# Position bias read bank by bank in the first block of a chunk, and two weight conversions one step sooner

## The chip, the cores and the metric

The program runs on one core of one Trainium2 chip. The metric is the device time of one execution in microseconds (us); the figure given is the median of several executions.

## The reference

Attention with a learned position bias, followed by a gated feed-forward layer (called MoE in the code, though there is one expert). Sizes: 4 batches, 8 heads, 576 positions, head width 64, 32 hidden units in the bias network, 2304 tokens, model width 512, inner width 1536. All inputs and outputs are float32.

```python
scores = q @ k.T / sqrt(64)
x = log1p(|i - j|) / log1p(max(i, 1))          # 576 x 576
bias = relu(x[..., None] @ w1 + b1) @ w2       # 576 x 576 x 8 heads
attn = softmax(scores + bias) @ v
x = attn, heads side by side                   # 2304 x 512
out = (sigmoid(x @ w_gate) * (x @ w_val)) @ w_out
```

## The kernel before

Three stages follow each other on the core: the position bias (up to about 115 us), attention (to about 348 us) and the MoE stage (to the end). Each engine works its instructions off in the order in which the program lists them; in all three stages this order is written out by hand (`tc.manual_schedule()`), and the tile framework adds a semaphore wait wherever an instruction uses a tile that another engine has written or read.

**The bias stage** (`bias`). Each hidden unit of the bias network is on or off at a position pair, so the bias is x times one sum over units plus another sum. The key positions are cut into 9 chunks of 64 (`NCH`; numbered 0 to 8 here), the query positions into 5 blocks of 128, taken in the order 0, 1, 4, 2, 3 (`BORD`). For each chunk and block TensorE sums the 0/1 tiles `ind` and `far` with the coefficients `cfs` into the PSUM tile `bps` (`sums`, L455). `bps` has two banks; bank a holds one half of the chunk's columns, and in each bank the first 256 values per partition are the sum that is multiplied by x, the other 256 the sum that is added. Two such tiles exist, so block 4, the third of a chunk, can start only when block 0 of that chunk has been read. `leave` (L457) empties a block. VectorE multiplies the first sums by x into `btmp` (L463). Then there are two ways for the second sums:

- blocks 1, 2 and 3: VectorE reads them and writes the bias itself (L474);
- block 0 of chunks 0 to 7 (`BPOOL`) and block 4: ScalarE copies them, scaled, to `brest` (L466), and GpSimd adds `brest` and `btmp` (L469). For block 4 the program lists ScalarE's read first and VectorE's read (L480) second.

Between these, ScalarE makes the `ind` tiles of the next chunk (L436, from the PSUM tile `y` that TensorE writes at L431), VectorE makes the `far` tiles (L449), a conversion of MoE weights runs on both (`cvm`; L229 on ScalarE, L232 to L241 on VectorE), and in chunks 3 to 6 TensorE adds 20 matmuls on the values of one batch to block 4 (`gram`, L379), which are loaded by DMA through GpSimd's queue.

**The MoE stage** (`Moe.run`). 24 steps, written in the string `ORDER`: A0 A1 B0 A2 B1 A3 ... (numbered 0 to 23). A step computes gate and value sums of one slice f of the inner width for one part of 384 tokens (TensorE L1024 into `pg` and `pu`); ScalarE takes the sigmoid (L1033), VectorE multiplies (L1034), ScalarE rounds the product to `gh` (L1035), VectorE subtracts for the rest `gl` (L1036). One step later TensorE multiplies `gh` and `gl` with the output weights (L1048, into `po`). `pg` and `pu` have one buffer each.

Weights are split in two parts before use, in tiles of 128x512: tile 3f+z is gate (z=0), value (z=1) or output weights (z=2) of slice f. ScalarE writes the upper part (L978) and, for a scale needed later, the sum of its squares (L997); VectorE writes the lower part (L987). Tiles 0 to 8 were converted in the bias stage, so for them this is all; tiles from 9 on first go through L229 (ScalarE), L232, L235, L238 and L241 (VectorE). Tile n is begun when its turn comes (`begin`): every step calls `convert`, which begins the next raw tile, moves the tiles already begun by one stage, and issues the load of another raw tile (`stage`, L955 or L958). Steps 2, 3, 4 and 9 call it once more (`EXTRA`). Ahead of that, the three strings of `START` say by hand what is done before step 0 and in steps 0 and 1: `s` issues one load from ScalarE's queue, `w5` does the next action of tile 5 (the sixth tile): first the upper part, then the lower part.

Of the kernel before, what the change touches and what calls it, by code (L numbers as in the profile page):

```python
# [15 lines left out]
AF = mybir.ActivationFunctionType  # L16
ALU = mybir.AluOpType

B, H, S, D = 4, 8, 576, 64
# [5 lines left out]
NCH = S // 64  # L25
# [11 lines left out]
BPOOL = (0,)  # L37
# [8 lines left out]
PRE = lambda f, z: f < 3  # L46
ORDER = "A0 A1 B0 A2 B1 A3 B2 A4 B3 A5 B4 A6 B5 A7 B6 A8 B7 A9 B8 A10 A11 B9 B10 B11"
CONV = (2, 1)
START = 'w2 w3 w3 w2 w4 s w4 s', 's s s s', 'w5 w5'
PLAN = {  # L50
# [195 lines left out]
def bias(tc, v, small, steps, lpos, xtab, lx, biases, biasL, ident, level, sizes, moe, begun):  # L246
# [4 lines left out]
    nc = tc.nc  # L251
    PSUM = bass.MemoryType.PSUM
    with ExitStack() as ph:
# [36 lines left out]
        ps = pp.tile([128, 2, 2, H, 32], F32, name="bps").rearrange("p a b h j -> p a (b h j)")  # L290
# [22 lines left out]
        for z, (o, col) in enumerate(((wl, 3), (wt, 7))):  # L313
            nc.vector.tensor_tensor(
                out=o, in0=wr[:, z].rearrange("p (o m) -> p o m", o=1).to_broadcast([128, 4, HID]),
                in1=pk[:, col:col + 4].rearrange("p (g o) -> p g o", o=1).to_broadcast([128, 4, HID]), op=ALU.mult)
        nc.vector.tensor_tensor(out=wl, in0=wl, in1=wt, op=ALU.add)
        for part in range(3):
# [9 lines left out]
            out=wy, in0=wt.rearrange("p (o g) m -> p o (g m)", o=1).to_broadcast([128, 4, 128]),  # L328
            in1=group.rearrange("p (r o) -> p r o", o=1).to_broadcast([128, 4, 128]), op=ALU.mult)
# [5 lines left out]
        for ab in range(2):  # L335
            nc.gpsimd.tensor_tensor(
                out=cf[:, ab], in0=w2r.rearrange("p (h o) -> p h o", o=1).to_broadcast([128, H, 4]),
                in1=group.rearrange("p (o g) -> p o g", o=1).to_broadcast([128, H, 4]), op=ALU.mult)
# [3 lines left out]
        total, cup, cun = (cp.tile([128, 1], F32, name=n) for n in ("ctotal", "cup", "cun"))  # L342
# [112 lines left out]
                nc.tensor.matmul(out=o, lhsT=st, rhs=cfs[:, part], start=(part == 0), stop=(part == 1))  # L455

        def leave(ps, c, blk):  # L457
            n = 2 if blk < 4 else 1
            tmp = tp.tile([128, 2, H, 32], F32, name="btmp")[:, 0:n]
            js = slice(64 * c, 64 * c + 64)  # L460
            if blk < 4:
                x = xt[:, blk, js].rearrange("p (s o j) -> p s o j", s=2, o=1)
                nc.vector.tensor_tensor(out=tmp, in0=ps[:, :, 0], in1=x.to_broadcast([128, 2, H, 32]), op=ALU.mult)  # L463
            if blk in BPOOL and c < NCH - 1 or blk == 4:
                rest = tp.tile([128, 2, H, 32], F32, name="brest")[:, 0:n]
                nc.scalar.activation(out=rest, in_=ps[:, 0:n, 1], func=AF.Copy, scale=cun)  # L466

                def put(out, in0, in1):
                    nc.gpsimd.tensor_tensor(out=out, in0=in0, in1=in1, op=ALU.add)  # L469
            else:  # L470
                rest = ps[:, 0:n, 1]

                def put(out, in0, in1):
                    nc.vector.scalar_tensor_tensor(out=out, in0=in0, scalar=cun, in1=in1, op0=ALU.mult, op1=ALU.add)  # L474
            if blk < 4:
                for t, h0, h1 in ((biases[0], 0, 6), (biases[1], 6, 8)):
                    put(t[:, :, blk::4, 32 * c:32 * c + 32], rest[:, :, h0:h1], tmp[:, :, h0:h1])
                return
            x = xt[:, 4, 64 * c:64 * c + 32].rearrange("p (o j) -> p o j", o=1)
            nc.vector.tensor_tensor(out=tmp[:, 0], in0=ps[:, 0, 0], in1=x.to_broadcast([128, H, 32]), op=ALU.mult)  # L480
            for s_ in range(2):
                r = slice(64 * s_, 64 * s_ + 64)
                for e in range(2):
                    put(biasL[64 * e:64 * e + 64, :, s_, 32 * c:32 * c + 32], rest[r, 0, e::2], tmp[r, 0, e::2])
# [16 lines left out]
        for c in range(NCH):  # L501
# [11 lines left out]
            for n, blk in enumerate(BORD):  # L513
                ps = pp.tile([128, 2, 2, H, 32], F32, name="bps")
# [322 lines left out]
class Moe:  # L837
# [442 lines left out]
    def run(self):  # L1280
# [4 lines left out]
        with ExitStack() as ph, tc.manual_schedule():  # L1285
# [14 lines left out]
            self.un, self.fits = {}, []  # L1300
            self.do(START[0], nc.scalar)
            before, opened = [], False
            for i, (c, f) in enumerate(order):
# [19 lines left out]
                if i < 2:  # L1323
                    self.do(START[1 + i], nc.scalar)
                for s in stored:
# [69 lines left out]
```

## Time and profile before

| | |
|---|---|
| median of 3 runs | 773.50 us (773.39 to 773.68) |
| the profiled execution, its own time | 772.53 us |
| its span, from first to last instruction | 770.7 us |
| TensorE busy | 716.0 us, 93% |
| VectorE busy | 630.3 us, 82% |
| ScalarE busy | 547.2 us, 71% |
| GpSimd busy | 343.2 us, 45% |
| mean granted TensorE clock over the span | 0.987 of full speed |

The profile is of one execution. A busy share is an average over three stages with different limits, so it says little of an edit in one stage; for that the timelines and the waits of the stretch in question are read. The bias stage lies at 12 to 115 us, the first steps of the MoE stage at 348 to 390 us. In a timeline a row gives the start, the duration, the engine, the line and the tiles (out<-in); in square brackets stands how long the engine had been idle and what it waited for.

### The profile page before, as it was taken

Reading aid. Unit: us, or ns where it says so; the run is one execution under the profiler, and the core shown is the slowest. Engines: PE = TensorE matmul, PEld = TensorE weight load, DVE = VectorE, ACT = ScalarE, POOL = GpSimd, SP = SyncE. Lnnn points to the kernel's source line nnn. Section 1 sums busy time; section 2 is a strip of 40 time slices with the busy share of each in tenths; the row PEclk is TensorE's granted clock in tenths of the full one; section 3 lists DMA queues with packets and bytes.
Section 4 is the critical chain, followed back from the end, with each engine's and each line's share of the span. In section 5 each row is a group of like instructions: output and inputs, shape, how many; then the busy total and the mean of one; then the engine's idle time right before and its main releaser. Section 6 shows DMA issues by size and latency. Waiting matters only on the chain.

```text
span 770.7 us, 16565 instructions
## 1 busy us (share of the span) xinstructions
PE 716.0 (93%) x6058; PEld 519.8 (67%) x6058; DVE 630.3 (82%) x1336; ACT 547.2 (71%) x1189; POOL 343.2 (45%) x436
## 2 busy tenths in 40 slices
PE   6877858999999998989999999999999999999997
PEld 3766746777777776769898999955555555555553
DVE  6788887999999999973789898879888886777662
ACT  5987737989889898875667565777766667566653
POOL 4343456998989999891000000125423340534200
PEclk9999987999999999999999999999999999999999
DMA  6387424878899789888687523345222213412102
GB/s 197 134 187 201 128 82 94 170 167 191 176 168 195 158 202 221 201 198 282 210 278 232 175 98 109 128 158 181 82 83 72 66 55 114 151 47 73 56 1 82
DMA packets 128593, 111.77 MB, mean 145 GB/s; under 512 B 78848, under 2 KB 99456, under 8 KB 128512
## 3 DMA queue, kind: packets, MB, share of 16 engines
q1 hardware_dynamic: 124480, 105.15, 50.0%
q0 software_dynamic: 2112, 2.62, 2.3%
q10 hardware_dynamic: 1920, 2.95, 1.1%
q8 instruction: 47, 0.77, 0.4%
q14 instruction: 34, 0.28, 0.1%
HBM read 76.08 MB, written 18.95 MB: 123 GB/s over the span
## 4 chain that ended last, share of the span: by engine, by line
PE 60%; DVE 9%; ACT 8%; DMA 3%; issue 3%; POOL 1%; SPq 0%; ACTq 0%; DVEq 0%; POOLq 0%
PE po L1048 16%; PE pg L1196 10%; PE pu L1196 7%; PE pg L1024 6%; PE pu L1024 6%; PE acc L768 5%; PE sc L660 4%; PE pt L705 3%; DVE en L676 3%; ACT at L590 3%; ACT en L681 2%; DVE at L591 2%; PE sc L649 1%; DMA vr<-in_v_dram 1%; DMA wo<-scratch 1%
## 5 line engine op out<-in xcount | busy, mean ns | idle before, releaser
L1154 POOL TENSOR_TENSOR ws<-wm 128x256 f32<-128x256 f32 x44 | 43.1, 979 | 283.6 <-DMA xt<-xs 145.1
L1196 PEld LDWEIGHTS <-wv 128*128 128x128 f16 x1008 | 98.0, 98 | 83.1 <-issue 8.2
L681 ACT ACTIVATE en<-en,mn 128x576 f32<-128x576 f32 x144 | 110.7, 774 | 17.0 <-DVE mn L676 16.6
L1196 PE MATMUL pg<-xq,wv 128*128 128x384 f16 x576 | 109.3, 326 | 2.5 <-ACT c L1222 2.1
L676 DVE CUSTOM_DVE_ANT_1 en<-sc,bias 128x576 f32<-128x576 f32 x128 | 91.7, 754 | 10.7 <-PE sc L660 10.2
L699 POOL TENSOR_TENSOR cr<-en,cr 128x512 f16<-128x512 f32 x124 | 90.0, 748 | 5.2
L1048 PE MATMUL po<-wo,gh 128*128 128x512 f16 x288 | 85.6, 379 | 0.0
L1196 PE MATMUL pu<-xq,wv 128*128 128x384 f16 x432 | 82.0, 326 | 1.1 <-DVE c L1202 0.9
L660 PE MATMUL sc<-k,part 64*128 64x288 f32 x768 | 77.3, 319 | 2.8 <-DVE bias L474 1.4
L591 DVE SCALAR_TENSOR_TENSOR at<-pt,at 128x512 f16<-128x512 f32 (+3 forms) x132 | 72.0, 565 | 7.9 <-ACT at L590 6.3
L1202 DVE TENSOR_TENSOR c<-pu,c 128x384 f32<-128x384 f32 x72 | 39.9, 554 | 42.7 <-PE pu L1196 28.0
L660 PEld LDWEIGHTS sc<-k,part 64*128 64x128 f32 x768 | 60.5, 191 | 19.0 <-issue 13.1
L590 ACT ACTIVATE at<-pt 128x512 f16<-128x512 f32 (+3 forms) x132 | 61.6, 493 | 9.5 <-PE pt L705 8.2
L768 PE MATMUL acc<-at,vv 128*64 128x288 f16 x868 | 65.8, 289 | 2.7 <-ACT xe L772 1.1
L455 PE MATMUL bps<-cfs,ind 128*128 128x64 f16 x972 | 52.6, 194 | 14.1 <-DVE bias L474 7.8
L436 ACT ACTIVATE ind<-y 128x576 bf16<-128x576 f32 x100 | 60.5, 650 | 6.4 <-PE y L431 5.8
L1214 ACT ACTIVATE gh<-c 128x384 f16<-128x384 f32 x48 | 25.1, 522 | 54.0 <-DVE c L1212 52.5
L455 PEld LDWEIGHTS <-ind 128*128 128x128 bf16 x972 | 45.4, 99 | 23.1 <-issue 10.8
L705 PE MATMUL pt<-ident,en 128*128 128x128 f32 x328 | 53.4, 286 | 7.8 <-ACT en L681 5.0
L768 PEld LDWEIGHTS <-vv 128*64 128x64 f16 x896 | 48.1, 109 | 17.2 <-issue 14.5
L1024 PE MATMUL pg<-xhi,w 128*128 128x384 f32 x192 | 53.9, 339 | 1.2 <-DVE w L987 1.0
L1048 PE MATMUL po<-wo,gl 128*128 128x512 f16 x144 | 54.6, 379 | 0.0
(194 smaller groups left out, 1678.3 us busy)
## 6 DMA issues: line engine op xcount, KB each, us to landing
wm<-scratch SPq DMA_DIRECT2D x48, 256.0 KB
scratch<-wm SPq DMA_DIRECT2D x27, 256.0 KB
wo<-scratch SPq DMA_DIRECT2D x24, 256.0 KB
qr<-in_q_dram SPq DMA_DIRECT2D x16, 320.0 KB
vr<-in_v_dram SPq DMA_DIRECT2D x16, 320.0 KB
kr<-in_k_dram SPq DMA_DIRECT2D x16, 288.0 KB
xs<-xe SPq DMA_DIRECT2D x16, 288.0 KB
xrec<-rs SPq DMA_DIRECT2D x48, 96.0 KB
```

The costliest lines, as they stand in the source:

```text
L455: nc.tensor.matmul(out=o, lhsT=st, rhs=cfs[:, part], start=(part == 0), stop=(part == 1))
L590: nc.scalar.activation(out=hi, in_=ps, func=AF.Copy, scale=float(2.0 ** up))
L591: return lambda: nc.vector.scalar_tensor_tensor(out=lo, in0=ps, scalar=float(2.0 ** up), in1=hi, op0=ALU.mult, op1=ALU.subtract)
L660: nc.tensor.matmul(out=pair[h][:, e, 0:HF], lhsT=qs[rows, l, 128 * it:128 * it + 128], rhs=ks[rows, r, HF * e:HF * e + HF], start=(i == 0) ...
L676: nc.vector.tensor_tensor_reduce(out=half(en), in0=ps[:, :, 0:HF], in1=nbias, scale=-0.125, scalar=3.0e38, op0=ALU.add, op1=ALU.min, accum ...
L681: nc.scalar.activation(out=en, in_=en, func=AF.Exp, bias=mn, scale=-1.0, accum_out=sm)
L699: nc.gpsimd.tensor_tensor(out=t[:, a:a + z.stop - z.start], in0=en[:, z], in1=t[:, z], op=ALU.subtract)
L705: nc.tensor.transpose(pt[:, J], en[:, 128 * J:128 * J + 128], ident)
L768: nc.tensor.matmul(out=acc[D * h:D * h + D, 0:HF], lhsT=vv[:, h, J, z], rhs=at[:, h, y, cs], start=(i == 0), stop=(i == len(mms) - 1))
L1024: self.nc.tensor.matmul(out=(pg, pu)[z], lhsT=l, rhs=r, start=(kc == 0 and i == 0), stop=(kc == 3 and i == 2))
L1048: self.nc.tensor.matmul(out=po, lhsT=l[:, tt], rhs=r, start=(first and i == 0), stop=(last and i == 2))
L1196: nc.tensor.matmul(out=p, lhsT=W[i][:, l, at + kc], rhs=V[b][:, r, kc], start=(new and n == 0), stop=(n == 5), skip_group_check=not new)
```

## The change

It has two parts.

1. In `leave`, for block 0 of chunks 0 to 7 (`apart`), VectorE's one read of 512 values (L463) becomes two of 256, one for each bank, and ScalarE's one copy of 512 values (L466) becomes two of 256. They are listed in turn: VectorE bank 0, ScalarE bank 0, VectorE bank 1, ScalarE bank 1. In the changed kernel these are L469 and L470. Block 4 runs through the same loop with one round, as before.
2. In `START`, `w5 w5` moves from step 1 to step 0 of the MoE stage, behind the four loads that ScalarE's queue issues there.

```diff
-START = 'w2 w3 w3 w2 w4 s w4 s', 's s s s', 'w5 w5'
+START = 'w2 w3 w3 w2 w4 s w4 s', 's s s s w5 w5', ''
...
         def leave(ps, c, blk):
-            n = 2 if blk < 4 else 1
+            n, apart = 2 if blk < 4 else 1, blk in BPOOL and c < NCH - 1
             tmp = tp.tile([128, 2, H, 32], F32, name="btmp")[:, 0:n]
             js = slice(64 * c, 64 * c + 64)
             if blk < 4:
                 x = xt[:, blk, js].rearrange("p (s o j) -> p s o j", s=2, o=1)
-                nc.vector.tensor_tensor(out=tmp, in0=ps[:, :, 0], in1=x.to_broadcast([128, 2, H, 32]), op=ALU.mult)
-            if blk in BPOOL and c < NCH - 1 or blk == 4:
+                if not apart:
+                    nc.vector.tensor_tensor(out=tmp, in0=ps[:, :, 0], in1=x.to_broadcast([128, 2, H, 32]), op=ALU.mult)
+            if blk == 4 or apart:
                 rest = tp.tile([128, 2, H, 32], F32, name="brest")[:, 0:n]
-                nc.scalar.activation(out=rest, in_=ps[:, 0:n, 1], func=AF.Copy, scale=cun)
+                for a in range(n):
+                    if apart:
+                        nc.vector.tensor_tensor(out=tmp[:, a], in0=ps[:, a, 0], in1=x[:, a].to_broadcast([128, H, 32]), op=ALU.mult)
+                    nc.scalar.activation(out=rest[:, a], in_=ps[:, a, 1], func=AF.Copy, scale=cun)
```

The change moves instructions at two places, shown as the built programs list them. Line numbers behind L457 are larger by 4 in the changed kernel.

The first place is block 0 of chunk 1, VectorE. In brackets stands which engine's semaphore an instruction waits on (Activation is ScalarE). Before:

```order
L449 TENSOR_TENSOR far<-dist,edge 128x2x512
L463 TENSOR_TENSOR btmp<-bps,xt 128x512 [waits PE_49]
L449 TENSOR_TENSOR far<-dist,edge 128x2x512
L463 TENSOR_TENSOR btmp<-bps,xt 128x512 [waits DVE_49,PE_49]
L474 SCALAR_TENSOR_TENSOR bias_72<-bps,cun,btmp 128x12x32 [waits DVE_49]
L474 SCALAR_TENSOR_TENSOR bias_73<-bps,cun,btmp 128x4x32
L232 TENSOR_SCALAR cvm<-cvm 128x512 [waits Activation_49]
```

and with the change:

```order
L449 TENSOR_TENSOR far<-dist,edge 128x2x512
L469 TENSOR_TENSOR btmp<-bps,xt 128x256 [waits PE_49]
L469 TENSOR_TENSOR btmp<-bps,xt 128x256 [waits Activation_49]
L449 TENSOR_TENSOR far<-dist,edge 128x2x512
L464 TENSOR_TENSOR btmp<-bps,xt 128x512 [waits DVE_49,PE_49]
L478 SCALAR_TENSOR_TENSOR bias_72<-bps,cun,btmp 128x12x32 [waits DVE_49]
L478 SCALAR_TENSOR_TENSOR bias_73<-bps,cun,btmp 128x4x32
```

ScalarE at the same place, before:

```order
L436 ACTIVATE ind_508<-y 128x576 [waits PE_49]
L436 ACTIVATE ind_509<-y 128x576 [waits PE_49,Activation_49]
L466 ACTIVATE brest<-bps,cun 128x512 [waits DVE_49,Activation_49,Pool_49]
L229 ACTIVATE cvm<-cvw 128x512 [waits DMAHW1_49]
L436 ACTIVATE ind_510<-y 128x576 [waits PE_49]
L436 ACTIVATE ind_511<-y 128x576 [waits PE_49]
```

and with the change:

```order
L436 ACTIVATE ind_510<-y 128x576 [waits PE_49]
L436 ACTIVATE ind_511<-y 128x576 [waits PE_49,Activation_49]
L470 ACTIVATE brest<-bps,cun 128x256 [waits DVE_49,Activation_49,Pool_49]
L470 ACTIVATE brest<-bps,cun 128x256 [waits DVE_49]
L229 ACTIVATE cvm<-cvw 128x512 [waits DMAHW1_49]
L436 ACTIVATE ind_512<-y 128x576 [waits PE_49]
L436 ACTIVATE ind_513<-y 128x576 [waits PE_49]
```

The second of VectorE's two reads waits for ScalarE, and the second of ScalarE's for VectorE: the four go one after the other. In chunks 1 to 7, TensorE's first matmul of block 4 waits for the last ScalarE read of block 0, in both kernels. The reads of chunks 0 and 2 to 7 are listed with the same waits.

The second place is the MoE stage. ScalarE from the last load of step 0 on (the name w2_1 is tile 5, w0_2 tile 6, w0_0 and w1_0 tiles 0 and 1; `room` receives squares that nobody reads), before:

```order
L958 DMA ww_6985<-in_moe_w_out_dram 128x1024
L997 ACTIVATE room_6925,squares_6924<-w0_0_6045 128x512
L997 ACTIVATE room_6925,squares_6924<-w1_0_6285 128x512
L978 ACTIVATE w2_1_7030<-ww_6940 128x512
L1033 ACTIVATE g_7034<-pg_6992 128x384
L1035 ACTIVATE gh_7035<-g_7034 128x384
L978 ACTIVATE w0_2_7041<-ww_6943 128x512
```

and with the change:

```order
L962 DMA ww_7001<-in_moe_w_out_dram 128x1024
L982 ACTIVATE w2_1_7003<-ww_6956 128x512
L1001 ACTIVATE room_6941,squares_6940<-w0_0_6061 128x512
L1001 ACTIVATE room_6941,squares_6940<-w1_0_6301 128x512
L982 ACTIVATE w0_2_7049<-ww_6959 128x512
L1001 ACTIVATE w0_2_7049,squares_6940<-w0_2_7049 128x512
L1037 ACTIVATE g_7054<-pg_7011 128x384
```

Tile 5 comes ahead of two sums of squares, and tile 6 ahead of step 1's sigmoid (L1033, now L1037). On VectorE tile 5's lower part now also stands ahead of step 0's `gl`.

VectorE from step 3's product on (ww_6981 and ww_6997 are tile 9, ww_6983 and ww_6999 tile 10), before:

```order
L1034 TENSOR_TENSOR g_7148<-pu_7106,g_7148 128x384
L232 TENSOR_SCALAR wm_7143<-wm_7143 128x512
L235 TENSOR_SCALAR wm_7143<-wm_7143 128x512
L238 SCALAR_TENSOR_TENSOR wm_7143<-ww_6981,wm_7143 128x512
L241 SCALAR_TENSOR_TENSOR wm_7143<-ww_6981,wm_7143 128x512
L232 TENSOR_SCALAR wm_7154<-wm_7154 128x512
L1036 TENSOR_TENSOR gl_7150<-g_7148,gh_7149 128x384
L1034 TENSOR_TENSOR g_7205<-pu_7171,g_7205 128x384
L235 TENSOR_SCALAR wm_7154<-wm_7154 128x512
L238 SCALAR_TENSOR_TENSOR wm_7154<-ww_6983,wm_7154 128x512
L241 SCALAR_TENSOR_TENSOR wm_7154<-ww_6983,wm_7154 128x512
L232 TENSOR_SCALAR wm_7159<-wm_7159 128x512
```

and with the change:

```order
L1038 TENSOR_TENSOR g_7167<-pu_7125,g_7167 128x384
L235 TENSOR_SCALAR wm_7116<-wm_7116 128x512
L238 SCALAR_TENSOR_TENSOR wm_7116<-ww_6997,wm_7116 128x512
L241 SCALAR_TENSOR_TENSOR wm_7116<-ww_6997,wm_7116 128x512
L232 TENSOR_SCALAR wm_7162<-wm_7162 128x512
L235 TENSOR_SCALAR wm_7162<-wm_7162 128x512
L238 SCALAR_TENSOR_TENSOR wm_7162<-ww_6999,wm_7162 128x512
L241 SCALAR_TENSOR_TENSOR wm_7162<-ww_6999,wm_7162 128x512
L232 TENSOR_SCALAR wm_7173<-wm_7173 128x512
L1040 TENSOR_TENSOR gl_7169<-g_7167,gh_7168 128x384
L1038 TENSOR_TENSOR g_7231<-pu_7197,g_7231 128x384
L991 TENSOR_TENSOR w0_3_7182<-wm_7116,w0_3_7182 128x512
```

Tile 9 comes out finished one step earlier and tile 10 right behind it. The next quartet on VectorE is then tile 11's; from step 5's product on, the order of VectorE's instructions is the same in both kernels. GpSimd's order is unchanged, and TensorE's too; on SyncE's queue the stores of converted tiles from tile 9 on stand one place further ahead among the loads of raw tiles.

## Rows read from the trace of the kernel before

**Rows 1.** The waits from 12 to 112 us: total us, times, longest.
```profile
ACT brest L466 <- DVE btmp L463: 10.3, 8, 2.6
...
DVE btmp L480 <- ACT brest L466: 8.7, 6, 3.7
...
PE bps L455 <- ACT brest L466: 5.6, 7, 1.0
```

**Rows 2.** Timeline, VectorE, chunk 4: start, duration, instruction, idle time before it.
```profile
59.73 0.68 DVE L463 TENSOR_TENSOR btmp<-bps,xt 128x512 f32<-128x512 f32 x1
...
64.61 0.42 DVE L480 TENSOR_TENSOR btmp<-bps,xt 128x256 f32<-128x256 f32 x1 [0.70 <-ACT brest L466]
```

**Rows 3.** Timeline, ScalarE, chunk 4.
```profile
60.52 0.69 ACT L466 ACTIVATE brest<-bps,cun 128x512 f32<-128x512 f32 x1 [0.85 <-DVE btmp L463]
...
64.03 0.47 ACT L466 ACTIVATE brest<-bps,cun 128x256 f32<-128x256 f32 x1
```

**Rows 4.** Timeline, TensorE, chunk 4.
```profile
61.26 0.28 PE L455 MATMUL bps<-cfs,ind 128*128 128x64 f16 x4 [0.75 <-ACT brest L466]
...
62.64 1.28 PE L379 MATMUL bps<-vb 128*128 128x128 bf16 x20
```

**Rows 5.** Timeline, TensorE, the first matmuls of the attention stage.
```profile
115.41 0.85 PE L660 MATMUL sc<-k,part 64*128 64x288 f32 x4 [1.38 <-DVE bias L474]
```

**Rows 6.** Timelines of ScalarE, TensorE, VectorE, chunk 5.
```profile
72.47 0.67 ACT L229 ACTIVATE cvm<-cvw 128x512 f32<-128x512 f32 x1 [0.58 <-DMA cvw<-in_moe_w_out_dram]
...
73.72 0.41 PE L431 MATMUL y<-lt,wy 128*128 128x288 bf16 x2 [1.51 <-ACT ind L436]
...
74.99 2.34 PE L379 MATMUL bps<-vb 128*128 128x128 bf16 x20
...
78.03 0.42 DVE L480 TENSOR_TENSOR btmp<-bps,xt 128x256 f32<-128x256 f32 x1 [3.70 <-ACT brest L466]
```

**Rows 7.** Busy us by stretch: PE, PEld, DVE, ACT, POOL, granted clock, DMA share, GB/s.
```profile
75.00:76.00 1.00, 1.00 (x11) 1.00 (x10) 0.00 (x0) 0.65 (x1) 0.00 (x0) 0.50 1.06 332
```

**Rows 8.** Timeline, TensorE, steps 1 to 6 of the MoE stage.
```profile
357.96 0.40 PE L1048 MATMUL po<-w,gl 128*128 128x512 f32 x1
...
359.59 0.34 PE L1024 MATMUL pg<-xhi,w 128*128 128x384 f32 x1
...
372.08 0.34 PE L1024 MATMUL pg<-xhi,w 128*128 128x384 f32 x1
...
379.87 0.62 PE L1024 MATMUL pg<-xhi,w 128*128 128x384 f32 x2 [1.00 <-DVE w L987]
...
383.07 0.62 PE L1024 MATMUL pu<-xhi,w 128*128 128x384 f32 x2 [0.84 <-DVE w L987]
...
387.23 0.45 PE L1024 MATMUL pg<-xhi,w 128*128 128x384 f32 x1
```

**Rows 9.** Timeline, ScalarE and its queue, step 1 of the MoE stage.
```profile
355.58 0.90 ACTq L958 DMA_DIRECT2D ww<-in_moe_w_out_dram  x1
...
356.53 0.63 ACT L997 ACTIVATE room<-w 128x512 bf16<-128x512 f32 x1 [2.23 <-DMA ww<-in_moe_w_val_dram]
...
357.92 0.62 ACT L978 ACTIVATE w<-ww 128x512 fp32r<-128x512 f32 x1
...
358.44 0.47 ACT L1033 ACTIVATE g<-pg 128x384 f32<-128x384 f32 x1
```

**Rows 10.** Timeline, VectorE, steps 3 to 5 of the MoE stage.
```profile
370.26 0.56 DVE L1034 TENSOR_TENSOR g<-pu,g 128x384 f32<-128x384 f32 x1 [1.81 <-PE pu L1024]
...
376.53 0.56 DVE L1034 TENSOR_TENSOR g<-pu,g 128x384 f32<-128x384 f32 x1 [2.66 <-PE pu L1024]
...
379.74 0.42 DVE L235 TENSOR_SCALAR wm<-wm 128x512 int32<-128x512 int32 x1
...
381.86 0.55 DVE L1036 TENSOR_TENSOR gl<-g,gh 128x384 fp32r<-128x384 f32 x1
...
387.78 0.55 DVE L1034 TENSOR_TENSOR g<-pu,g 128x384 f32<-128x384 f32 x1
```

## The prediction

> **What bounds the kernel now.** The change touches two stages, so I read those two and nothing of the 230 us of attention between them. First the summed waits of the bias stage [rows 1]. ScalarE waits eight times, once for each chunk from 0 to 7, for VectorE's read of block 0 before it may copy the other half of the tile. TensorE waits seven times for that copy, 0.8 us on average. VectorE waits for ScalarE's copy of block 4, 8.7 us in all. Each wait hands over to the next, so block 0 lies on a ring: VectorE reads, ScalarE copies, TensorE fills block 4, ScalarE copies block 4, VectorE reads it and goes on to the next chunk.
>
> The timelines of one chunk show the ring in times. VectorE reads block 0 from 59.73 for 0.68 us [rows 2]. ScalarE was idle for 0.85 us and starts 0.11 us after that read ends, at 60.52, for 0.69 us [rows 3]. TensorE was idle for 0.75 us and starts 0.05 us after that copy, at 61.26 [rows 4]. The copy of block 4 runs from 64.03 to 64.50 [rows 3], and VectorE, idle for 0.70 us, reads block 4 at 64.61 [rows 2]. Whoever gets longer between 59.73 and 61.21 delays the whole chunk. At the end the first scores of attention wait 1.38 us for the last bias that VectorE writes [rows 5], so a delay of the bias stage is handed on whole.
>
> In the MoE stage TensorE is nearly always busy. The stretch to look at is steps 4 and 5: two steps take 359.59 to 372.08, 12.49 us, where nothing is late, and the next two take 372.08 to 387.23, 15.15 us, where TensorE waits for VectorE's lower parts of tiles 9 and 10 [rows 8]. That is 2.66 us which an earlier conversion could win.
>
> **Part 1, the reads of block 0.** The pieces of 256 values are in the trace, as block 4 is read in just this form: 0.42 us on VectorE [rows 2], 0.47 us on ScalarE [rows 3]. A hand-over between the two takes 0.11 us either way. The listing shows that the second read of each engine waits for the other engine, so the four reads stand in a row.
>
> - Before: 0.68 + 0.11 + 0.69 = 1.48 us (59.73 to 61.21).
> - After: 0.42 + 0.11 + 0.47 + 0.11 + 0.42 + 0.11 + 0.47 = 2.11 us.
>
> So ScalarE ends 0.63 us later in each chunk, and TensorE, which already waits there, starts block 4 0.63 us later. ScalarE's `ind` tiles queue behind its second copy and move by as much. VectorE cannot go on while it waits: its second read ends 1.53 us after the start of the first instead of 0.68, so all behind it on VectorE is 0.85 us later. At block 4 VectorE had 0.70 us to spare [rows 2], which takes that down to 0.15, less than the 0.63 that reaches it from ScalarE. GpSimd's additions wait for the second copy, but GpSimd is idle then.
>
> Eight chunks would give 5.0 us. In chunk 5 ScalarE waits 0.58 us for a weight load anyway, just behind its copy [rows 6]; the load was issued a chunk earlier and moves with what came before, but chunk 5's own 0.63 falls almost whole into that wait. I take 7 x 0.63 + 0.05 = **4.5 us slower**. The bounds: if VectorE's second read did not wait, ScalarE's two copies would take between 0.69 (as one) and 0.94 (end to end), say 0.82, and the row becomes 0.42 + 0.11 + 0.82 = 1.35 us, which is 8 x 0.13 = 1.0 us faster; if VectorE has nothing to spare, 8 x 0.85 = 6.8 us slower. I take the value between because the rows of chunk 4 show which wait ends last.
>
> The Trainium skill, PSUM — Partial Sum Buffer, section "PSUM bank collisions raise a hardware error", says that two engines may read different banks at once and need a guard only for the same bank. By that, nothing in the chip asks VectorE's read of bank 1 to wait for ScalarE's read of bank 0, and the sum would end at the lower bound just given. The listing has the wait nevertheless, and the engines obey the listing.
>
> **Part 2, tile 5 one step sooner.** `w5 w5` used to be a lower part only, since `convert` in step 1 had begun tile 5. Now both actions come in step 0, `convert` in step 1 begins tile 6 instead, and each tile up to 11 is done earlier. No work is added; what counts is who queues behind it.
>
> - Step 0: ScalarE's queue is busy with loads until 355.58 + 0.90 = 356.48 [rows 9], so the upper part of tile 5 comes at 356.53 and ends at 357.14 (0.62 us). VectorE's lower part, some 0.7 us, now stands ahead of `gl`, which takes 0.55 us [rows 10] and so ends at about 358.35. TensorE wants it at 357.96 [rows 8]: 0.4 us of waiting.
> - Step 1: ahead of the sigmoid ScalarE now has tile 5's and tile 6's upper parts (0.52 us each from start to start), two sums of squares (356.53 to 357.92, 1.39 us) and a third that needs tile 6 (some 0.7 us) [rows 9]: it starts at about 359.75 instead of 358.44 and ends at 360.2. `pg` has one buffer, and TensorE wants it at 359.59 [rows 8]. So step 2 starts 0.7 us late, the 0.4 us included.
> - Steps 3 to 5 on VectorE: before, from step 3's product at 370.26 to step 5's at 387.78 lie 17.52 us with 2.66 us idle in them [rows 10], 14.9 us of work. The change has the same instructions there but one L232 fewer, 14.5 us. It starts 0.7 us later, at 370.96. Two quartets of 2.12 us (379.74 to 381.86) and two products follow, done by 376.2; step 4's sums come at 376.53 + 0.7, so about 1.0 us stays idle. Step 5's product then comes at 370.96 + 14.5 + 1.0 = 386.4, **1.4 us sooner**. TensorE's two waits vanish: tile 9's lower part follows step 4's product and is ready at 377.2 + 0.5 + 0.7 = 378.4, wanted at 379.87 - 1.00 + 0.7 = 379.6 [rows 8]; tile 10's follows a quartet later, ready at 378.4 + 2.1 + 0.7 = 381.2, wanted at 383.07 - 1.84 + 0.7 = 381.9.
>
> From step 5 on VectorE's order is as before and it stays nearly full, so I take VectorE's 1.4 us as the gain and not TensorE's 2.66 - 0.7. Bounds: 0 if tile 5's load lands later than 357 (its wait is hidden before), 2.66 if neither new wait shows.
>
> **The sum.** 4.5 - 1.4 = 3.1 us slower. The profiled execution took 772.53 us and would take 775.6; the median stands 0.97 us above it, so 773.5 + 3.1 = **776.6 us**. About 0.2%, 1.5 us, is what a measurement of this kernel can tell from no change; the boundaries are 771.95 and 775.05.
>
> **The rivals.**
>
> 1. *The clock falls in another chunk, 778.5 us, chance 0.20.* In chunk 5 TensorE stood idle for 1.51 us shortly after its wait for block 0, the granted clock went to 0.50, the 1.2 GHz level [rows 6, 7], and the 20 matmuls took 2.34 us instead of 1.28 [rows 4, 6]. With 0.63 us more idle time for each chunk, chunks 6 and 7 may fall too, at 1.06 us or a little less each: 1.9 us more. Against it: in the other chunks TensorE is soon busy again.
> 2. *The delay is swallowed, 774.6 us, chance 0.10.* Chunk 5 has 3.70 us of idle VectorE [rows 6]; if what it waits for comes at a fixed time, the delays of chunks 0 to 4 are lost in it: 3.1 less two to three chunks' 0.63. Against it: GpSimd issues those loads behind its additions, which move as well.
> 3. *Part 2 gains nothing, 778.0 us, chance 0.10.* Tile 5's load or a buffer is late, and steps 0 to 2 lose what steps 4 and 5 win: 4.5 alone.
> 4. *The reads overlap, 771.1 us, not slower, chance 0.08.* One mechanism: VectorE's wait is for something long done, so bank 1 is read while ScalarE reads bank 0. Then part 1 is the lower bound, 1.0 us faster, and with part 2 the sum is -2.4. It decides if VectorE's second read starts less than 0.4 us after its first. The skill's rule on banks named above would allow it. Against it: ScalarE waits for VectorE's read of a whole tile in all eight chunks now [rows 1], though the halves are different values, so the framework guards tiles and not values.
>
> **How the numbers follow.** My own case has 0.52. The range 774.2 to 779.2 us takes in that case, rivals 1 to 3 and the nearer part of the unknown costs; outside lie rival 4 and several clock falls or full 0.85 us chunks together. Faster by over 0.2%: 0.07, nearly all rival 4. Within 0.2%: 0.16, rival 2 and the low edge of my case. Slower by over 0.2%: 0.77.
>
> **What would show it.** Right: in each chunk 0 to 7 VectorE's second read starts about 1.1 us after the first with a wait for ScalarE; TensorE's waits for that copy sum to some 10 us instead of 5.6; attention's first scores come near 120 us instead of 115.41; in the MoE stage the waits for tiles 9 and 10 are gone, and new ones of about 0.4 and 0.3 us stand in steps 1 and 2. Wrong: second reads back to back, a bias stage of the old length, or more clock at 0.50 than before.

## The result, and the profile after

| | before | changed |
|---|---|---|
| median of 10 executions each, taken side by side | 773.44 us | 779.12 us |
| lowest and highest | 771.77, 774.99 | 775.63, 781.11 |
| the profiled execution, its own time | 772.53 us | 776.28 us |
| its span | 770.7 us | 774.3 us |

The ratio is 1.0068, 95% interval 1.0051 to 1.0085: 3.9 to 6.6 us slower. The forecast was 776.6 us and slower, and the median lies 0.08 us inside the upper end of its range. The profiled execution is only 3.6 us longer in its span than the one of before, close to the 3.1 us of the sum, so two questions follow: whether the terms come out as worked, and what the other executions have that this one has not.

First the summed waits of the bias stage in the changed kernel, 12 to 112 us, as in [rows 1].

```profile
ACT brest L470 <- DVE btmp L469: 11.6, 15, 2.0
PE bps L455 <- ACT brest L470: 9.0, 7, 1.5
DVE btmp L484 <- ACT brest L470: 5.4, 5, 2.5
DVE btmp L469 <- ACT brest L470: 4.9, 8, 0.6
```

The last line is new: VectorE's second read waits for ScalarE eight times, 0.6 us each. TensorE's seven waits for ScalarE's copy sum to 9.0 us instead of 5.6. Now the timeline of chunk 4, VectorE, then ScalarE, then TensorE, which answers to [rows 2 to 4].

```profile
62.10 0.42 DVE L469 TENSOR_TENSOR btmp<-bps,xt 128x256 f32<-128x256 f32 x1
63.15 0.42 DVE L469 TENSOR_TENSOR btmp<-bps,xt 128x256 f32<-128x256 f32 x1 [0.62 <-ACT brest L470]
63.49 0.68 DVE L238 SCALAR_TENSOR_TENSOR cvm<-cvw,cvm 128x512 int32<-128x512 int32 x1
...
67.48 0.42 DVE L484 TENSOR_TENSOR btmp<-bps,xt 128x256 f32<-128x256 f32 x1 [0.40 <-ACT brest L470]
...
62.64 0.47 ACT L470 ACTIVATE brest<-bps,cun 128x256 f32<-128x256 f32 x1 [0.58 <-DVE btmp L469]
63.60 0.47 ACT L470 ACTIVATE brest<-bps,cun 128x256 f32<-128x256 f32 x1 [0.49 <-DVE btmp L469]
...
64.13 0.28 PE L455 MATMUL bps<-cfs,ind 128*128 128x64 f16 x4 [1.24 <-ACT brest L470]
```

The four reads stand in a row, from 62.10 to 64.07: 1.97 us, where it was 1.48. TensorE waits 1.24 us, where it was 0.75. That is 0.49 us for the chunk, and VectorE keeps 0.40 us of its 0.70 us at block 4.

One stretch shows what the forecast's own case did not have. In chunk 2 TensorE stood idle for 1.50 us ahead of block 4 (before: 1.02 us), and some 2 us later its clock fell. The rows of TensorE's timeline, before and changed:

```profile
40.26 0.28 PE L455 MATMUL bps<-cfs,ind 128*128 128x64 f16 x4 [1.02 <-ACT brest L466]
...
41.04 0.28 PE L455 MATMUL bps<-cfs,ind 128*128 128x64 f16 x4 [1.50 <-ACT brest L470]
```

And windows of the changed kernel: busy time of PE, PEld, DVE, ACT and POOL, then the granted clock, the share of the DMA engines and GB/s.

```profile
38.00:43.30 5.30, 3.13 (x61) 2.44 (x61) 4.64 (x11) 3.61 (x8) 2.23 (x3) 1.00 0.50 151
43.70:46.20 2.50, 2.50 (x37) 2.15 (x35) 1.15 (x3) 1.78 (x4) 1.79 (x4) 0.50 0.76 88
...
340.00:342.00 2.00, 1.84 (x9) 1.19 (x9) 1.74 (x6) 2.00 (x7) 1.92 (x3) 0.57 1.06 224
342.00:344.00 2.00, 2.00 (x21) 1.48 (x22) 0.69 (x1) 2.00 (x7) 1.91 (x4) 0.58 0.80 250
```

At 0.50 (1.2 GHz) that interval took 12.30 us from block 4 to block 4 instead of 10.70. The same happened late in attention, at 340 to 344 us. Before, the clock was 1.00 at both places. In both kernels it is also low for a longer time where the bias stage passes into attention, so that stretch is no difference between them. Windows inside it, before and changed:

```profile
112.00:125.00 13.00, 10.89 (x76) 8.45 (x75) 8.11 (x22) 5.96 (x12) 5.37 (x9) 0.50 0.17 49
...
119.00:129.00 10.00, 8.81 (x47) 6.80 (x49) 5.80 (x18) 5.90 (x12) 3.86 (x5) 0.52 0.06 13
```

In the MoE stage TensorE has one new wait, in step 1, and none for tiles 9 and 10. Timeline rows of the start of step 2 and of step 6, and the first matmul of the stage:

```profile
354.24 0.44 PE L1028 MATMUL pg<-xhi,w 128*128 128x384 f32 x1
...
364.15 0.50 PE L1052 MATMUL po<-w,gl 128*128 128x512 f32 x1 [0.43 <-DVE gl L1040]
...
366.07 0.41 PE L1028 MATMUL pg<-xhi,w 128*128 128x384 f32 x1
...
391.33 0.33 PE L1028 MATMUL pg<-xhi,w 128*128 128x384 f32 x1
```

So the 3.6 us split up like this. The scores of attention that wait for the last bias come at 119.46 us instead of 115.41 [rows 5] (+4.05). The MoE stage starts at 354.24 instead of 348.63, so attention is 1.56 us longer. The slow stretch at 340 us lies in it, but that is not all: in a second profile of the change, shown below, there is no such stretch, and attention is still 1.08 us longer than before. Why was not looked up. The MoE stage takes 774.3 - 354.24 = 420.06 us instead of 422.07 (-2.01). The row of the scores in the changed kernel, and the first matmul of the MoE stage before:

```profile
119.46 1.78 PE L664 MATMUL sc<-k,part 64*128 64x288 f32 x11 [1.82 <-DVE bias L478]
...
348.63 0.44 PE L1024 MATMUL pg<-xhi,w 128*128 128x384 f32 x1
```

### The profile page after: what moved, and what is told of

The parts are those of the page before. It is cut to its first block, busy times and chain, and to the rows that moved or that the text cites. A ratio compares the mean times of both kernels' runs of the same rounds, so it can differ in the third digit from the quotient of the medians.

```text
span 774.3 us, 16577 instructions
## 1 busy us (share of the span) xinstructions
PE 717.2 (93%) x6058; PEld 520.2 (67%) x6058; DVE 629.6 (81%) x1344; ACT 550.1 (71%) x1197; POOL 342.4 (44%) x436
## 4 chain that ended last, share of the span: by engine, by line
PE 59%; DVE 9%; ACT 8%; DMA 5%; issue 2%; POOL 1%; SPq 1%; ACTq 0%; DVEq 0%; POOLq 0%
PE po L1052 16%; PE pg L1200 10%; PE pu L1200 7%; PE pg L1028 6%; PE pu L1028 6%; PE acc L772 5%; PE sc L664 4%; PE pt L709 3%; DVE en L680 3%; ACT at L594 3%; ACT en L685 2%; DVE at L595 2%; DMA xrec<-rs 2%; PE sc L653 1%; DMA vr<-in_v_dram 1%
```

## The experiments

The theories. **A**: each part costs what the profile shows, the length of the hand-over chain in part 1 and the earlier conversions in part 2. **B**: part 2 is to blame for the longest executions. **C**: they come from a TensorE clock that falls in some chunks of some executions, after the longer idle stretches. **D**: part 2 gains nothing in the end. **E**: what costs is that VectorE is held between its two reads. **F**: behind the hand-over stands another wait of the same length.

### Each part by itself

Part 1 alone is the change with `START` of before; part 2 alone is the kernel before with the new `START`.

Part 1 alone:

> Only the reads of block 0 are changed; the MoE stage starts as in the kernel before. Theory A (each part costs what the profile of the change shows: bias stage about 4 us longer, MoE stage 1.5 to 2 us shorter): 773.4 + 4 to 5.5 = 777.5 to 779, the first scores of attention near 119.5 us, the waits for tiles 9 and 10 (1.0 and 0.8 us) back. Rival B (the change's slower runs near 780.8 come from part 2, for example from loads that collide late in the MoE stage): 776 to 777, with no runs above 779. Rival C (the slower runs come from a TensorE clock that falls in some executions after the longer idle stretches of the bias stage): runs spread over some 4 us, up to 783, and the granted clock of the profile is at its lower level in chunks where it was not before.

Part 2 alone:

> Only the START strings are changed; block 0 is read as before. Theory A: 1.5 to 2 us faster than before, 771.5 to 772, with waits of 0.4 us for gl in step 1 and none for tiles 9 and 10, and no wider spread than the kernel before. Rival B (part 2 is to blame for the slower runs): at or above 773.5, with runs in two groups some 3 to 4 us apart. Rival D (VectorE's later steps give the gain back, since they stay full): 773.4, no difference.

Measured: part 1 alone 779.92 us, ratio 1.0095 (1.0074 to 1.0117), above the 777.5 to 779 of A; part 2 alone 771.79 us, 0.9985 (0.9971 to 1.0). B falls: the part that costs is the first, and part 2 gains about 1.4 us, though its interval reaches to no difference. D is not favoured. The profile of part 1 alone was of an execution of 780.51 us, and shows falls as C has them: the clock was at its lower level in chunks 1, 5, 6 and 7 and late in attention. Windows inside each of these stretches, columns as above:

```profile
33.00:35.00 2.00, 2.00 (x29) 1.72 (x28) 0.73 (x2) 1.50 (x3) 1.41 (x3) 0.50 0.00 0
77.00:79.00 2.00, 2.00 (x22) 1.82 (x20) 0.77 (x3) 1.06 (x2) 0.87 (x1) 0.50 0.99 261
91.00:93.00 2.00, 2.00 (x20) 1.91 (x19) 0.71 (x3) 0.65 (x1) 0.00 (x0) 0.50 0.00 0
108.00:110.00 2.00, 2.00 (x28) 1.63 (x26) 1.83 (x5) 1.03 (x2) 1.77 (x4) 0.50 0.33 131
343.00:346.00 3.00, 2.88 (x19) 1.94 (x19) 1.94 (x6) 3.00 (x10) 2.83 (x5) 0.50 1.06 218
```

### The change once more

> The change itself once more, beside the others on the same chip, for its spread and a second profile. Theory A alone: 776 to 778 in all runs. Rival C: again two groups, near 776 to 777.6 and near 780.8, and the granted clock of this profile is low in another set of chunks than in the first profile of the change (chunks 2 to 3, chunk 5 and attention at 340 to 344 us).

Measured: 778.21 us, 1.0070 (1.0044 to 1.0095), executions from 776.02 to 781.14. They fill the space between, so "two groups" was too strong; the spread was right. The profiled execution, of 776.02 us, has its clock falls in chunks 6 and 7, and none in chunks 2 and 5 nor at 340 us. Its chunk 6, TensorE, then the scores that wait for the last bias, and the start of the MoE stage:

```profile
87.69 0.28 PE L455 MATMUL bps<-cfs,ind 128*128 128x64 f16 x4 [1.51 <-ACT brest L470]
...
89.22 2.34 PE L379 MATMUL bps<-vb 128*128 128x128 bf16 x20
...
120.57 1.77 PE L664 MATMUL sc<-k,part 64*128 64x288 f32 x11 [1.20 <-DVE bias L478]
...
354.87 0.44 PE L1028 MATMUL pg<-xhi,w 128*128 128x384 f32 x1
```

The same program, so which chunks fall is not fixed by it. The time from VectorE's read of block 4 in one chunk to that in the next, read off the timelines; * marks an interval with a stretch at the lower clock:

| to chunk | 1 | 2 | 3 | 4 | 5 | 6 | 7 | 8 |
|---|---|---|---|---|---|---|---|---|
| before | 10.20 | 10.41 | 10.70 | 10.97 | 13.42* | 11.48 | 11.11 | 10.55 |
| change | 10.74 | 10.87 | 12.30* | 11.46 | 12.97* | 11.97 | 11.90 | 10.89 |
| change again | 10.75 | 10.88 | 11.18 | 11.46 | 11.98 | 13.19* | 11.89* | 11.42* |
| part 1 alone | 10.74 | 11.67* | 11.17 | 11.46 | 13.40* | 13.50* | 11.88 | 11.42* |
| both, then both | 10.41 | 10.95 | 10.91 | 11.20 | 12.78* | 11.71 | 11.18 | 10.64 |

The columns to chunks 1, 2, 3 and 4 without a star show the bare price of part 1: 0.46 to 0.55 us, and the same in all three profiles to 0.01 us. A fall adds 0.5 us (to chunk 8, part 1 alone) to 1.5 us (to chunk 6, part 1 alone). In these words a fall is named by the chunk whose matmuls it slows, so one behind block 4 of chunk 2 lengthens the interval to chunk 3.

To chunk 7 the price without a fall is higher, 0.77 to 0.79 us. There TensorE waits once for a value that VectorE makes (`vmost`), so VectorE's delay counts as well. Before and changed:

```profile
99.76 0.16 PE L396 MATMUL bps<-vmost,ones 128*128 128x1 bf16 x1 [1.16 <-DVE vmost L394]
...
103.46 0.16 PE L396 MATMUL bps<-vmost,ones 128*128 128x1 bf16 x1 [1.46 <-DVE vmost L394]
```

To chunk 8, where no read is split, the change takes 0.34 us more; the cause was not looked up.

The length of the idle stretch alone does not decide whether the clock falls. In all three profiles TensorE stands idle for 1.50 or 1.51 us ahead of block 4 in chunks 2, 5 and 6, and the clock fell behind five of these nine stretches: chunks 2 and 5 of the change, 6 of the change again, 5 and 6 of part 1 alone. Part 1 alone has a fall in chunk 1 with no stretch over 0.82 us in the 10 us before it.

### Pieces without turns

```diff
-                for a in range(n):
-                    if apart:
-                        nc.vector.tensor_tensor(out=tmp[:, a], ...)
-                    nc.scalar.activation(out=rest[:, a], ...)
+                for a in range(n):
+                    if apart:
+                        nc.vector.tensor_tensor(out=tmp[:, a], ...)
+                for a in range(n):
+                    nc.scalar.activation(out=rest[:, a], ...)
```

> Reads of 256 values as in the change, but listed as VectorE bank 0, VectorE bank 1, ScalarE bank 0, ScalarE bank 1, so VectorE never waits for ScalarE in between; START as before. By the rows, pieces of one engine start 0.34 (VectorE) and 0.37 us (ScalarE) apart: 0.34 + 0.42 + 0.11 + 0.37 + 0.47 = 1.71 us from VectorE's first start to ScalarE's end, against 1.48 before and 1.97 measured in the change. Theory A (pieces cost 0.23 us and turns 0.26 us for each chunk): 8 x 0.23 = 1.8 us, 775.2. If the turns cost everything: 773.4. If the number of pieces costs everything: as e1, 777.5 or more. Rival C adds that runs spread less than in e1, as TensorE's idle stretch is shorter by 0.26 us.

Measured: 775.62 us, 1.0030 (1.0013 to 1.0046). In its profile, chunk 4, the two reads of each engine run as one piece:

```profile
60.37 0.74 DVE L469 TENSOR_TENSOR btmp<-bps,xt 128x256 f32<-128x256 f32 x2
...
61.23 0.84 ACT L471 ACTIVATE brest<-bps,cun 128x256 f32<-128x256 f32 x2 [0.91 <-DVE btmp L469]
...
62.12 0.28 PE L455 MATMUL bps<-cfs,ind 128*128 128x64 f16 x4 [0.97 <-ACT brest L471]
```

From 60.37 to 62.07 are 1.70 us, against 1.48 and 1.97. So of the 0.49 us of this chunk 0.22 is the number of pieces and 0.27 the turns, as theory A had it. The intervals agree to chunks 1, 3 and 4 (0.21, 0.21 and 0.23 us longer than before) and not to chunk 2 (0.54), where ScalarE starts 0.44 us after VectorE's second read instead of 0.12; why is open. Up to block 4 of chunk 8 this profile has no clock fall but the one in chunk 5.

### The chain longer in another way, and VectorE later without the chain

ScalarE copies block 0 twice (kernel before):

```diff
-                nc.scalar.activation(out=rest, in_=ps[:, 0:n, 1], func=AF.Copy, scale=cun)
+                for _ in range(n):
+                    nc.scalar.activation(out=rest, in_=ps[:, 0:n, 1], func=AF.Copy, scale=cun)
```

> The kernel before, but ScalarE copies the second half of block 0 (and block 0 of no other kind) twice into the same brest tile: TensorE's block 4 waits some 0.6 us longer in chunks 0 to 7, VectorE's reads are as before and VectorE isn't held. Theory A (only the length of the chain up to ScalarE's last copy counts, whatever makes it longer): each undisturbed chunk 0.5 to 0.6 us longer, bias stage 4 us longer less what chunk 5 takes up, with clock falls in more chunks than chunk 5 in some executions: 777 to 780. Rival E (the change costs by holding VectorE between its two reads, 0.85 us of it in each chunk): 773 to 774 here.

Measured: 780.76 us, 1.0086 (1.0063 to 1.0108), just above the 777 to 780 expected. Its intervals to chunks 3 and 4 are 11.45 and 11.68, 0.75 and 0.71 us longer than before, more than the 0.6 expected; to chunk 1 it is 11.35, 1.15 us longer without a fall, which the doubled copy alone does not explain. The clock fell in chunks 1, 6 and 7. So a longer chain is enough for a loss like the change's, with nobody's reads taking turns and VectorE not held, against E.

VectorE multiplies once more behind its read of block 0, into a spare tile (kernel before):

```diff
+                if blk in BPOOL and c < NCH - 1:
+                    more = tp.tile([128, 2, H, 32], F32, name="bmore")
+                    nc.vector.tensor_tensor(out=more, in0=tmp, in1=x.to_broadcast([128, 2, H, 32]), op=ALU.mult)
```

> The kernel before, with one more multiplication of 512 values on VectorE right behind its read of block 0 in chunks 0 to 7 (SBUF to a spare tile, read by nobody): VectorE is 0.6 us later behind the read, the chain to ScalarE and TensorE is not touched. Theory A (VectorE's slack of 0.70 us at block 4 takes this up): chunk lengths within 0.1 us of before in most chunks, 773 to 774.5. Rival E (holding VectorE is what costs): 8 x 0.6 = 4.8 us, 778.

Measured: 779.54 us, 1.0065 (1.0043 to 1.0086). This looked like E. The rows of chunk 4 (VectorE, then GpSimd) show another cause:

```profile
61.35 0.68 DVE L463 TENSOR_TENSOR btmp<-bps,xt 128x512 f32<-128x512 f32 x1
62.07 0.69 DVE L466 TENSOR_TENSOR bmore<-btmp,xt 128x512 f32<-128x512 f32 x1
62.68 0.69 DVE L238 SCALAR_TENSOR_TENSOR cvm<-cvw,cvm 128x512 int32<-128x512 int32 x1
63.28 1.50 DVE L449 TENSOR_TENSOR far<-dist,edge 128x1024 bf16<-128x1024 f16 x1
...
67.01 0.42 DVE L483 TENSOR_TENSOR btmp<-bps,xt 128x256 f32<-128x256 f32 x1
...
62.98 2.12 POOL L472 TENSOR_TENSOR bias<-brest,btmp 128x384 f32<-128x384 f32 x2 [4.50 <-ACT brest L469]
```

The `far` tile takes 1.50 us instead of 0.68. It starts while GpSimd is adding, which the delay of 0.6 us brought about; six of the chunks have it. VectorE's account of the interval to chunk 4: 10.97 us before, less its idle 0.70 [rows 2] and 0.25 us (ahead of its read of block 2), plus 0.60 for the extra work and 0.82 for the slow `far`, is 11.44; measured 11.40. To chunk 1, where no `far` is slow, the extra work costs 0.07 us (10.27 against 10.20). There the slack at block 4 takes the delay up. The profiled execution is the fastest of the six, at 776.18 us; what makes the others longer was not profiled.

### What the hand-over is worth, and the slow tiles taken out

ScalarE's copy for block 0 reads x from SBUF, so the second sums of block 0 are left out of the bias, and nothing is handed over:

> The kernel before, but ScalarE's copy for block 0 reads 512 values of another tile (x, in SBUF), so it leaves the second sums of block 0 out of the bias; VectorE alone has to read the tile and ScalarE doesn't wait for it. This prices what reads at the same time could win at most. Theory A: TensorE's 5.6 us of waiting for the copy in seven chunks go, 0.4 to 0.8 us for each chunk: 768 to 770. Rival F (another wait of nearly the same length stands right behind, for example for ind tiles, and takes its place): 772 to 773.

Measured: 773.48 us, 0.9995 (0.9979 to 1.0010), no gain. TensorE's waits for the copy are gone, and those for VectorE's bias tiles (first line: before the change 7.8 us) have grown; six `far` tiles took 1.50 us here too.

```profile
PE bps L455 <- DVE bias L474: 13.6, 19, 2.1
```

To take the slow tiles out, GpSimd's additions for block 0 were listed behind those for block 4 in four kernels, with block 0's products in a tile of their own:

```diff
+                def adds():
+                    for t, h0, h1 in ((biases[0], 0, 6), (biases[1], 6, 8)):
+                        put(...)
+                if blk in BPOOL and c < NCH - 1:
+                    held.append(adds)
+                else:
+                    adds()
...
+            while held:
+                held.pop(0)()
```

The kernel before with later additions:

> Control: the kernel before, with GpSimd's two additions for block 0 listed behind its additions for block 4, and block 0's products in a tile of their own. In the kernel before the additions slow no far tile (0.68 us each), so theory A': no difference, 773 to 774, far tiles 0.68 us.

With the extra multiplication:

> VectorE's extra multiplication with GpSimd's additions later. In the profile of the run with the extra multiplication six far tiles took 1.50 us instead of 0.68, in the chunks where they started while GpSimd was adding; 6 x 0.82 = 4.9 us. Theory A' (VectorE's slack at block 4 takes up the 0.6 us, and the 5 us came from the slowed far tiles): far tiles 0.68 us again, 774 to 775.5. Rival E (holding VectorE behind block 0 costs by itself): 778 to 779 as before.

With the copy from SBUF:

> ScalarE's copy for block 0 reads x (second sums of block 0 left out of the bias), with GpSimd's additions later. In the profile without the second part six far tiles took 1.50 us here too. Theory A' (the hand-over is worth 0.4 to 0.8 us for each chunk, and the slowed far tiles took it back): 769 to 770. Rival F (another wait takes its place: TensorE's waits for VectorE's bias tiles were 13.6 us instead of 7.8): 772 to 773.5 as before.

Measured: control 777.12 us, 1.0039 (1.0021 to 1.0056); with the extra multiplication 781.57, 1.0099 (1.0082 to 1.0117); with the copy from SBUF 770.49, 0.9958 (0.9940 to 0.9976). The `far` tiles took 0.7 us again in all three. But the control was not neutral, a miss: the additions now fall on conversions, and `cvm` (L235) went from 415 to 597 ns on average. So the other two are compared with the control.

The copy from SBUF gains 6.6 us there, so the hand-over is worth something. Part of it is the clock: the control's profile has a fall in chunk 6, and this one has none up to block 4 of chunk 7. F holds in part: TensorE's waits for VectorE's bias tiles are 13.3 us here and 9.2 in the control. That the slow tiles had eaten the gain without a change of the additions is argued, not shown: here VectorE's conversions (L232 to L241 in the kernel before) take 5.1 us more in all than there, and the six slow `far` tiles had cost 4.9.

The extra multiplication costs 4.5 us more than the control in the median, against A'. In the profiles it costs 0.01, 0.15 and 0.01 us in the intervals to chunks 1, 2 and 5, which hold no fall in either (10.21, 11.18, 11.97; control 10.20, 11.03, 11.96). To chunk 7, also without a fall, it costs 0.73 (11.76; 11.03), and TensorE's wait for `vmost` grows by just that, from 1.16 to 1.89 us. To chunks 3 and 4, where it has a fall and the control has none, it costs 1.41 and 2.18. So holding VectorE costs by itself in chunk 7, as E has it; elsewhere the loss lies in the intervals with a fall, and why the clock falls there was not tested.

### A version faster than both

ScalarE alone empties block 0, in one copy of 1024 values, and GpSimd does the multiplication as well; with the new `START`:

```diff
+                if alone:
+                    both = tp.tile([128, 2, 2, H, 32], F32, name="bboth")
+                    nc.scalar.activation(out=both, in_=ps, func=AF.Copy, scale=cun)
+                    nc.gpsimd.tensor_tensor(out=both[:, :, 0], in0=both[:, :, 0], in1=x.to_broadcast([128, 2, H, 32]), op=ALU.mult)
+                    tmp, rest = both[:, :, 0], both[:, :, 1]
```

> Meant to beat both: the START strings of the change, and block 0 of chunks 0 to 7 is emptied by ScalarE alone, in one copy of 1024 values; GpSimd multiplies the first half by x (which is left unscaled there, as the copy scales both halves) and adds as before. From the copies of 256 (0.47 us) and 512 values (0.69) one of 1024 should take 1.13 us; ScalarE sits idle from 59.67 in chunk 4 and would end at 60.83 instead of 61.21. Theory A: 0.38 us for each chunk, 3 us less, and 1.4 for part 2: 768.5 to 769.5. Against it: GpSimd has some 1.2 us more work for each chunk and its loads of v come later (then 770 to 772), or VectorE and TensorE wait elsewhere and the bias stage stays as long as before (771.8).

Measured: 768.96 us, 0.9934 (0.9913 to 0.9954), as expected. The copy in ScalarE's timeline:

```profile
46.42 1.11 ACT L469 ACTIVATE bboth<-bps,cun 128x1024 f32<-128x1024 f32 x1
```

TensorE's waits for it, summed over 12 to 112 us:

```profile
PE bps L455 <- ACT bboth L469: 0.8, 3, 0.4
```

One engine reads the tile, so there is nothing to hand over: 0.8 us of waiting are left of 5.6. Part of that comes back elsewhere: the waits for VectorE's bias tiles are 10.1 us instead of 7.8. In this profile all of the gain stands ahead of the MoE stage, which starts at 345.46 us and then takes 422.04 us, as long as before. The wait for `gl` in step 1 was 1.10 us and took part of what the new `START` wins; where the rest went was not looked up.

With GpSimd's work for block 0 later as well:

> ScalarE alone empties block 0 (with the START strings of the change), and GpSimd's multiplication and additions for block 0 are listed behind those for block 4. Three far tiles were slow there (1.08 to 1.76 us), some 2 us in all, and some conversions too. Theory A': up to 2 us faster than without the second part, 767 to 768.5. Against it: the work now falls on other instructions of VectorE, and block 0's tile is held longer: 769 to 771.

Measured: 771.50 us, 0.9970 (0.9953 to 0.9988): slower than without, as the control had warned.

## Why the prediction was right, and where it was off

- **Direction and chain.** Slower, for the reason given: the second read waits, the four reads stand in a row, TensorE waits longer. The row was worked out as 2.11 us and took 1.97, since only the first hand-over takes 0.12 us; those that follow take 0.04 and 0.03 (63.11 to 63.15, 63.57 to 63.60). So a chunk costs 0.49 us and not 0.63.
- **VectorE's slack.** The forecast let 0.15 us of VectorE's 0.85 reach block 4, against 0.63 from ScalarE, which leaves 0.48 us of slack there; measured 0.40. VectorE goes on 0.79 us later, not 0.85, and block 4 reaches it 0.49 later: 0.70 - 0.79 + 0.49 = 0.40. That ScalarE's copy is still what VectorE waits for in chunk 4 is in the rows above. In chunk 7 the forecast left out a path: TensorE waits for VectorE's `vmost`, and 0.30 us more are lost.
- **The sum of part 1.** 4.5 us forecast, 4.05 measured at the first scores, but made up differently: less for each chunk, 0.45 us won and not 0.05 lost in chunk 5 (with a fall in both profiles), 0.30 us for `vmost`, and about 1.1 us for a clock fall in chunk 2 to 3.
- **Part 2.** The waits came where they were put: 0.43 us for `gl` (forecast 0.4), step 2 late by 366.07 - 359.59 - 5.61 = 0.87 us (forecast 0.7), tiles 9 and 10 gone. Step 6 starts at 391.33 instead of 387.23, 4.10 us later where the stage began 5.61 later: 1.5 us won, forecast 1.4. The rest of the stage wins 0.5 more. Alone, part 2 gains 1.4 us in the medians. The second new wait, 0.3 us ahead of step 2, is not recorded as one; the first matmul of step 2 starts 0.40 us after the last one with output weights, before 0.23. And the delay of step 2 is not fixed: 0.03 us in the second profile of the change, 0.38 in part 2 alone, 1.57 in the kernel with ScalarE alone.
- **What failed** is the sum's step from one profile to the median, 3.1 us forecast and 5.7 measured. The own case had the clock fall in chunk 5 as before and nowhere else, and gave the other possibility 0.20 as rival 1, for chunks 6 and 7. The forecast named "more clock at 0.50 than before" as a sign of being wrong, and it came: both profiles of the change have two falls in the bias stage and part 1 alone has four, in varying chunks: 2, 5, then 6 and 7, then 1, 5, 6 and 7. Each execution has a mean granted clock on record: over the sixteen of the change, in both measurements, its median is 0.979, and over the 23 of the kernel before that were taken beside the second one it is 0.987. That TensorE's idle stretch ahead of block 4 would reach some 1.5 us, the length that stood ahead of the fall in chunk 5 before [rows 6], was to be seen: 1.02 us plus the 0.63 of the sum.
- **What stays open** is how much of the gap the falls explain. The profiled executions of the change are among its fastest, and none of 780 us or more was profiled. Part 1 alone at 780.51 us, with four falls and one in attention, is the nearest, but its MoE stage takes 421.98 us, 1.9 more than in the change; with the new `START` it would be at about 778.6, an estimate from these two stages. Nor does the mean granted clock tell long executions of the change from short ones: the six above 780 us have 0.976 to 0.980, the eight below 778 have 0.978 to 0.987, and 776.02 us was reached at 0.978.
- **Luck.** That the median lies inside the range is owed to the room left in it for rivals, and by 0.08 us it is luck; rival 1's 778.5 us comes nearer than the own case's 776.6, though its falls are neither fixed to chunks 6 and 7 nor of one price.
- **Rivals 2 to 4** fell. The delay is not swallowed, as 4.05 us of it reach attention; part 2 gains; and the second read starts 1.05 us after the first, not under 0.4. No run had two engines read two banks of one tile at once.

## What to carry to other kernels

Before splitting reads between two engines, look in the listing whether the second piece waits for the other engine, and count the pieces and the hand-overs: here both cost, and nothing ran at the same time. Why the second read has to wait for a read of the other bank was not tested; the halves in two separate tiles would be the test. Where a chain sets the pace, letting one engine do both halves can beat a split; here it took the 1.48 us down to 1.11. A term that lengthens TensorE's idle stretches should be priced with the clock it may cost, and a median set against one profile needs that term.

## What had not been expected of the hardware

- The clock falls are not fixed by the program: two profiles of one kernel have them in different chunks, while the intervals to chunks 1 to 4 without a fall repeat to 0.01 us. An idle stretch of the same 1.50 us stands ahead of a fall in five cases of nine.
- A `far` tile that starts while GpSimd adds took 1.48 to 1.52 us instead of 0.68, six of them in each of two kernels. It started 0.30 us after GpSimd's addition in the rows above, and 0.03 to 0.35 us after it in the twelve. VectorE's reads of PSUM at the same time kept their 0.68 us. The Trainium skill, SBUF — State Buffer, section "SBUF: two separate sides", says that VectorE and GpSimd share a pair of ports under an exclusive lock, held for a whole instruction, and that an operation of VectorE with two SBUF inputs needs it against one of GpSimd that reads SBUF. The trace agrees: 0.80 to 0.84 us are lost each time, and no `far` tile of 1024 values at whose start GpSimd was not adding was slow in these two kernels. The longer GpSimd's lead, the longer its two additions took, from 1.86 us at 0.03 to 2.15 at 0.35, so GpSimd too seems to be held at first; this was not tested.
- Of three hand-overs in a row the first took 0.12 us and the next two 0.04 and 0.03; why the first is longer is open.
